# Attention scores in 64-key blocks side by side, with a PSUM bank of their own, in a fused recurrence and feed-forward kernel

## The chip, the cores and the metric

The kernel runs on one core of one Trainium2 chip. The time is the device time of one execution in microseconds. The kernel before takes 698.79 us (median of 3 runs, 698.2 to 699.16). A core has a matrix engine (TensorE, in the profile PE for its matmuls and PEld for its weight loads), VectorE (DVE), ScalarE (ACT), GpSimd (POOL) and SyncE (SP, which issues most DMAs here). TensorE writes into PSUM, eight banks of 512 fp32 values on each of 128 partitions; DVE and ACT read them out.

## What is computed

```python
# per batch (4), head (8): 768 tokens, 48 features
a = (a_re + i a_im) * min(|a|, 0.999) / (|a| + 1e-6)
for t in range(S):
    state = diag(a[t]) @ state + outer(k[t], v[t])     # complex
    y[t]  = q[t] @ Re(state)
x   = y as (3072 tokens, 384)
out = (x @ w_a) * (x @ w_b) @ w_out                     # d_ff = 1536
```

The running product of the decays turns the recurrence into causal attention in chunks: with q and k scaled by the products up to their token (real and imaginary part stacked, 96 rows a head), the scores of a chunk are k·q for keys not later than the query, plus a state that carries the earlier chunks.

## The kernel before

A unit is one chunk of 128 tokens for two batches; there are 12 units, 6 chunks by 2 pairs of batches. For each unit three kinds of work follow one another:

- *Preparation* (`prep`, `scale`): DVE and ACT make the scaled q and k of the unit in `qk`; SP's DMAs (`stack`, L352) restack them to 96 rows a head in `stk`. DVE's stream of 128x768 and 128x1536 operations is here.
- *Attention* (`attn`), in pieces, for the two batches i of the unit and for the two groups hg of four heads. `scores` (L380): four fp32 matmuls, keys by queries 128x128, into one PSUM tile of the pool `ps_m` (two banks, which `transposes` and `state` use too), then DVE multiplies by the causal mask into `am` (L388). `transposes` (L392): keys of four heads to token rows, copied by ACT into `kt` (L400). `outputs` (L403): v times masked scores, plus the state times q, into `xp`; these matmuls use 32 columns of the array each, four column groups side by side (L425, `tile_position`). ACT rounds `xp` into `xh`, DVE makes the rest `xl` (L429, L434). `state` (L436): kt times v (L442), added to the state `us` by DVE (L449).
- *Feed-forward* of the unit: for each of 12 blocks f of d_ff, `gemm1` (L480) makes a and b in one PSUM tile of the pool `ps_ab` (three banks) with 18 matmuls of rounded fp32 (L486); ACT copies a out (L494), DVE multiplies (L495), ACT and DVE split the product into `hh` and `hl` (L496, L497), and `gemm2` (L500) adds six matmuls (L504) into the two output banks.

The feed-forward of unit w, the attention of unit w+1 and the preparation of unit w+3 run in one loop over f; `attn` is a generator that hands out its pieces in the list `order` (L455, and L459 for unit 0), one or more per slot of the loop. The attention of unit 0 stands alone ahead of the loop. In the first 120 us the weights are also converted, with two matmuls each (L150, L151) into a bank of `ps_ab` or `ps_m`.

A scheduler of the framework puts the instructions of each engine in order, by priority and by its own estimate of when operands are ready. `tc.high_priority(offset=...)` moves the reading of PSUM forward: ATTN_FIRST for the masks and copies of the attention, MOE_FIRST for the feed-forward. On the chip each engine works off its queue in that order, and a waiting instruction holds up all behind it.

Each v tile (L360, 128 tokens by 4 pairs of heads by 128 columns) holds an even head in the first 64 columns of a pair and an odd one in the other 64.

Of the kernel before, what the change touches and what calls it, by code (L numbers as in the profile page):

```python
# [70 lines left out]
def tile_kernel(ctx: ExitStack, tc: tile.TileContext, a_d, qk_d, v_d, w_d, qn_d, kn_d, vn_d, an_d, out_d):  # L71
# [9 lines left out]
    vpool = fast.enter_context(tc.tile_pool(name="vpool", bufs=2))  # L81
    kvp = fast.enter_context(tc.tile_pool(name="kvp", bufs=2))
    moe = fast.enter_context(tc.tile_pool(name="moe", bufs=2))
    ps_ab = fast.enter_context(tc.tile_pool(name="ps_ab", bufs=3, space=PSUM))
    ps_o = fast.enter_context(tc.tile_pool(name="ps_o", bufs=1, space=PSUM))
    ps_x = fast.enter_context(tc.tile_pool(name="ps_x", bufs=1, space=PSUM))
    ps_m = fast.enter_context(tc.tile_pool(name="ps_m", bufs=2, space=PSUM))


    ident = const.tile([128, 128], F32, name="ident")  # L90
    make_identity(nc, ident)
    mask = const.tile([128, 128], F32, name="mask")
    nc.gpsimd.memset(mask, 1.0)
    nc.gpsimd.affine_select(out=mask, in_=mask, pattern=[[1, 128]], compare_op=ALU.is_ge,
                            fill=0.0, base=0, channel_multiplier=-1)
    biases = const.tile([128, 6], F32, name="biases")
    b_tiny, b_sq, b_eps, b_one, b_inv, b_rsq = (biases[:, i:i + 1] for i in range(6))
    vec.memset(b_tiny, TINY)
# [32 lines left out]
    def split_weights():  # L131
        for f in range(NF):
            for m, (c0, n) in enumerate(WPART):
                raw = raws[f, m]
                t = moe.tile([128, n], F32, name="o_sb", bufs=O_BUFS)
                tu = t.bitcast(U32)
                vec.tensor_scalar(out=tu, in0=raw[:, :, 1], scalar1=3, scalar2=0x3FFFFFFF,
                                  op0=ALU.logical_shift_left, op1=ALU.bitwise_and)
                vec.scalar_tensor_tensor(out=tu, in0=raw[:, :, 0], scalar=29, in1=tu,
                                         op0=ALU.logical_shift_right, op1=ALU.bitwise_or)  # L140
                vec.scalar_tensor_tensor(out=tu, in0=raw[:, :, 1], scalar=0xC0000000, in1=tu,  # L141
                                         op0=ALU.bitwise_and, op1=ALU.bitwise_or)
                w_t[f, m] = wpool.tile([128, 2, n], F32, name=f"w{m}{f}")
                hi, lo = w_t[f, m][:, 0], w_t[f, m][:, 1]
                act.copy(out=r(hi), in_=t)
                if f < CONV_ON_AB:
                    lp = ps_ab.tile([128, 512], F32, name="ab")
                else:
                    lp = ps_m.tile([128, 512], F32, name="pm")
                pe.matmul(out=lp[:, 0:n], lhsT=ident, rhs=t, start=True, stop=False)  # L150
                pe.matmul(out=lp[:, 0:n], lhsT=r(nident), rhs=r(hi), start=False, stop=True)  # L151
                act.copy(out=r(lo), in_=lp[:, 0:n])
            yield
# [49 lines left out]
    def prep(u):  # L203
# [52 lines left out]
        cc, bb = c_t[:], b_t[:]  # L256

        def joined(out, x, y, n):
            pb = small.tile([128, 2, 2, NG], F32, name="pb")
            vec.tensor_tensor(out=pb[:, :, :, 0:n], in0=x,  # L260
                              in1=y.unsqueeze(1).broadcast_to([128, 2, 2, n]), op=ALU.mult)
            vec.tensor_tensor(out=out, in0=pb[:, :, 0, 0:n], in1=pb[:, :, 1, 0:n], op=ALU.add)
# [108 lines left out]
    def attn(u, xh, xl):  # L371
# [7 lines left out]

        def scores(i, hg):  # L380
            qs, ks = cols(i)
            sp = ps_m.tile([128, 4, 128], F32, name="pm")
            for h4 in range(4):
                h = hg * 4 + h4
                pe.matmul(out=sp[:, h4], lhsT=stk[:, h, ks], rhs=stk[:, h, qs], start=True, stop=True)  # L385
            am = kvp.tile([128, 512], F32, name="am", bufs=2).rearrange("p (h t) -> p h t", h=4)
            with tc.high_priority(offset=ATTN_FIRST):
                vec.tensor_tensor(out=am, in0=sp, in1=mask[:].unsqueeze(1).broadcast_to([128, 4, 128]),  # L388
                                  op=ALU.mult)
            ams[i, hg] = am  # L390

        def transposes(i, hg):  # L392
            qs, ks = cols(i)
            tp = ps_m.tile([128, 512], F32, name="pm")
            for h4 in range(4):
                pe.transpose(out=tp[:, h4 * KS:(h4 + 1) * KS], in_=stk[0:KS, hg * 4 + h4, ks],  # L396
                             identity=ident[0:KS, 0:KS])
            kt = kvp.tile([128, 4, KS], F32, name="kt", bufs=2)
            with tc.high_priority(offset=ATTN_FIRST):
                act.copy(out=kt.rearrange("p h k -> p (h k)"), in_=tp[:, 0:4 * KS])  # L400
            kts[i, hg] = kt

        def outputs(i, half):  # L403
# [32 lines left out]
        def state(i, hg):  # L436
# [10 lines left out]
            with tc.high_priority(offset=ATTN_FIRST):  # L447
# [4 lines left out]
                if rescaled(c):  # L452
                    vec.tensor_tensor(out=uv, in0=uv, in1=sv, op=ALU.mult)

        order = [(scores, 0, 0), (scores, 0, 1), (transposes, 0, 0), (transposes, 0, 1),  # L455
                 (outputs, 0, 0), (outputs, 0, 1), (scores, 1, 0), (residual, 0, 0), (state, 0, 0), (scores, 1, 1),
                 (state, 0, 1), (transposes, 1, 0), (transposes, 1, 1), (outputs, 1, 0),
                 (outputs, 1, 1), (state, 1, 0), (residual, 1, 0), (state, 1, 1)]
        if u == 0:  # L459
            order = [(scores, 0, 0), (scores, 0, 1), (outputs, 0, 0), (outputs, 0, 1), (scores, 1, 0), (scores, 1, 1),  # L460
                     (residual, 0, 0), (outputs, 1, 0), (outputs, 1, 1), (transposes, 0, 0), (transposes, 0, 1),
                     (residual, 1, 0), (state, 0, 0), (state, 0, 1), (transposes, 1, 0), (transposes, 1, 1),
                     (state, 1, 0), (state, 1, 1)]
        for fn, i, g in order:
            if not (last and fn in (transposes, state)):
                fn(i, g)
# [297 lines left out]
```

## Time and profile before

| | us |
|---|---|
| median of 3 runs (lowest, highest) | 698.79 (698.2, 699.16) |
| the profiled execution, its own time | 698.89 |
| span of its profile | 697.2 |
| PE busy, whole span | 655.2 |
| DVE busy | 551.8 |
| ACT busy | 308.9 |
| matmuls of the scores (L385): 384 passes, mean length of one | 0.279 |
| matmuls of the outputs (L425): 768 + 640 passes, mean | 0.277, 0.273 |
| mask (L388): 48 on DVE, mean | 0.685 |
| copy of kt (L400): 40 on ACT, mean | 0.477 |

A matmul's length in a profile runs from its start to its modelled end, and matmuls are pipelined: one starts long before the one ahead has ended. What PE really spends on a run of matmuls is seen from the distance between starts, or in the chain of work that ended last, where each row lasts until the next one takes over. "Idle before" in the groups of lines is time in which an engine had nothing running, with the engine and line that ended it. The 40 slices show each engine's busy share in tenths.

### The profile page before, as it was taken

What the parts mean: (1) busy time and instruction counts of PE and PEld (TensorE: products, weight loads), DVE (VectorE), ACT (ScalarE), POOL (GpSimd) and SP (SyncE); (2) the same over time, 40 slices, a digit from 0 to 9 for tenths busy, and PEclk for the clock granted to TensorE, in tenths of its full rate; (3) what the DMA queues carried; (4) which work ended last, traced back from release to release, by engine and by line L of the source; (5) the groups of instructions that cost most, each with busy time, mean ns of one, the idle gap of its engine ahead of it and who ended that gap; (6) DMA issues with size and microseconds to landing.
All of it is one profiled execution on the core that took longest, in us unless ns stands there. A gap on an engine that the chain in (4) does not pass through costs nothing.

```text
span 697.2 us, 14316 instructions
## 1 busy us (share of the span) xinstructions
PE 655.2 (94%) x5854; PEld 610.8 (88%) x5854; DVE 551.8 (79%) x1241; ACT 308.9 (44%) x618; POOL 5.6 (1%) x11
## 2 busy tenths in 40 slices
PE   3557999999999999999999999999999999999996
PEld 1224889899899999999999999999999999999996
DVE  5999899988888889989899898999989853232221
ACT  6357755634535445245363554535542332221221
POOL 3000000000000000000000000000000000000000
PEclk9567999999999999999999999999999999999999
DMA  8973202411414205134151340511510500400000
GB/s 312 402 291 108 79 1 54 129 55 55 128 42 130 81 28 149 60 98 129 25 160 46 102 134 1 169 67 47 145 46 2 165 25 17 106 24 2 24 1 28
DMA packets 32088, 63.94 MB, mean 92 GB/s; under 512 B 3984, under 2 KB 10640, under 8 KB 32016
## 3 DMA queue, kind: packets, MB, share of 16 engines
q1 hardware_dynamic: 28560, 58.23, 27.0%
q10 hardware_dynamic: 3456, 4.72, 1.9%
q8 instruction: 48, 0.79, 0.5%
q14 instruction: 24, 0.20, 0.1%
HBM read 39.32 MB, written 4.72 MB: 63 GB/s over the span
## 4 chain that ended last, share of the span: by engine, by line
PE 64%; DVE 27%; ACT 4%; DMA 2%; issue 1%; SPq 1%; ACTq 0%; DVEq 0%
PE ab L486 30%; PE o L504 14%; PE xp L425 6%; PE pm L385 5%; PE pm L442 4%; DVE a_t L292 3%; DVE pr L230 2%; DVE qk L312 2%; DVE h_t L495 2%; PE pm L396 2%; DVE hl L497 2%; PE pm L150 2%; DVE z L297 2%; DVE pb L260 1%; DVE z L236 1%
## 5 line engine op out<-in xcount | busy, mean ns | idle before, releaser
L486 PE MATMUL ab<-xh,w 128*128 128x256 f32 x1728 | 339.0, 285 | 0.0
L486 PEld LDWEIGHTS ab<-xh,w 128*128 128x128 f32 x1728 | 278.1, 190 | 1.8 <-issue 1.4
L486 PE MATMUL ab<-xl,w 128*128 128x256 f32 x864 | 245.1, 284 | 0.0
L486 PEld LDWEIGHTS ab<-xl,w 128*128 128x128 f32 x864 | 164.4, 190 | 0.5 <-issue 0.2
L504 PE MATMUL o<-w,hh 128*128 128x384 f32 x576 | 152.3, 344 | 0.0
L494 ACT COPY h_t<-ab 128x256 f32<-128x256 f32 x144 | 53.1, 369 | 176.9 <-PE ab L486 176.8
L495 DVE TENSOR_TENSOR h_t<-ab,h_t 128x256 f32<-128x256 f32 x144 | 60.5, 420 | 72.5 <-ACT h_t L494 72.3
L504 PEld LDWEIGHTS o<-w,hh 128*128 128x128 f32 x576 | 96.8, 190 | 3.7 <-issue 3.0
L504 PE MATMUL o<-w,hl 128*128 128x384 f32 x288 | 96.9, 336 | 0.0
L496 ACT CAST hh<-h_t 128x256 fp32r<-128x256 f32 x144 | 58.0, 403 | 81.1 <-DVE h_t L495 80.9
L497 DVE TENSOR_TENSOR hl<-h_t,hh 128x256 fp32r<-128x256 f32 x144 | 60.5, 420 | 17.5 <-ACT hh L496 17.3
L150 PE MATMUL ab<-o_sb,ident 128*128 128x384 f32 x42 | 29.1, 794 | 29.9 <-DVE o_sb L141 29.8
L385 PE MATMUL pm<-stk 128*128 128x128 f32 x384 | 54.4, 279 | 2.7 <-DMA stk<-qk 2.7
L504 PEld LDWEIGHTS o<-w,hl 128*128 128x128 f32 x288 | 54.1, 188 | 0.0
L385 PEld LDWEIGHTS pm<-stk 128*128 128x128 f32 x384 | 48.7, 191 | 5.9 <-issue 4.8
L230 DVE TENSOR_TENSOR pr<-z 128x384 f32<-128x384 f32 (+1 forms) x91 | 47.1, 524 | 2.4 <-ACT z L216 0.8
L150 PEld LDWEIGHTS ab<-o_sb,ident 128*128 128x128 f32 x42 | 10.2, 286 | 39.8 <-DVE o_sb L141 29.4
L292 DVE TENSOR_TENSOR a_t<-z,b_t 128x768 f32<-128x768 f32 x48 | 44.6, 952 | 0.1
L425 PE MATMUL xp<-am,v_t 128*32 128x128 f32 x768 | 42.5, 277 | 1.3 <-DVE am L388 1.2
L312 DVE TENSOR_TENSOR qk<-qk,z 128x1536 f32<-128x1536 f32 (+1 forms) x28 | 42.7, 1524 | 0.1
L388 DVE TENSOR_TENSOR am<-pm,mask 128x512 f32<-128x512 f32 x48 | 32.8, 685 | 5.0 <-PE pm L385 4.8
L425 PE MATMUL xp<-stk,u 128*32 128x128 f32 x640 | 34.4, 273 | 0.0
(106 smaller groups left out, 761.7 us busy)
## 6 DMA issues: line engine op xcount, KB each, us to landing
w<-in_dram SPq DMA_DIRECT2D x36, 384.0 KB, 8.1
qk<-in_dram SPq DMA_DIRECT2D x12, 768.0 KB, 4.8
a_t<-in_dram SPq DMA_DIRECT2D x11, 768.0 KB, 4.3
stk<-qk SPq DMA_DIRECT2D x42, 192.0 KB, 3.3
v_t<-in_dram SPq DMA_DIRECT2D x24, 256.0 KB, 2.7
out_dram<-o_sb ACTq DMA_DIRECT2D x24, 192.0 KB, 1.9
stk<-qk SPq DMA_DIRECT2D x18, 192.8 KB, 3.4
stk<-qk SPq DMA_DIRECT2D x14, 128.0 KB, 3.1
```

What stands on the lines that cost most here:

```text
L150: pe.matmul(out=lp[:, 0:n], lhsT=ident, rhs=t, start=True, stop=False)
L230: vec.tensor_tensor(out=pr[:, :, :, o:o + n], in0=view(zz, W + at_(i) + 2 * o, [[W, 2], [-W, 2], [2, n]]), in1=tok(slice(1, 3), i - 1, o, ...
L292: vec.tensor_tensor(out=pz[:, s].rearrange("p (j b e) -> p j b e", j=SUB // 2, e=2), in0=zb[:, 1 + s], in1=view(bb, (1 + k - s) * NB, [[0, ...
L312: vec.tensor_tensor(out=qk4[:, :, k, x0:x1], in0=qk4[:, :, 1, x0:x1], in1=z[:, k].rearrange("p (j t) -> p j t", j=NJ).unsqueeze(2).broadca ...
L385: pe.matmul(out=sp[:, h4], lhsT=stk[:, h, ks], rhs=stk[:, h, qs], start=True, stop=True)
L425: pe.matmul(out=xp[qd * 32:(qd + 1) * 32, ti], lhsT=l, rhs=rr, start=st, stop=sp_, tile_position=(0, qd * 32), skip_group_check=True)
L486: pe.matmul(out=ab[:, m * TOK:(m + 1) * TOK], lhsT=r(w_ab(f, part, m * NJ + i)), rhs=r(xt[:, i, :]), start=n == 0, stop=n == 8)
L494: act.copy(out=h_t, in_=ab[:, 0:TOK])
L495: vec.tensor_tensor(out=h_t, in0=ab[:, TOK:2 * TOK], in1=h_t, op=ALU.mult)
L496: act.copy(out=r(hh), in_=h_t)
L497: vec.tensor_tensor(out=r(hl), in0=h_t, in1=hh, op=ALU.subtract)
L504: pe.matmul(out=os_[tt][:, 0:DM], lhsT=r(ht[:, ts]), rhs=r(w_t[f, 2][:, part, :]), start=(f == 0 and n == 0), stop=(f == NF - 1 and n == 2))
```

## The change

Scores are made in two blocks b of 64 keys. Block 0 meets all 128 queries, block 1 only the queries 64 to 127; the block of later keys and earlier queries is left out. Each matmul uses 64 columns of the array, and an even and an odd head work in the two column halves at once: half g = b xor x, x being 0 for the even head. An odd head's two halves of keys therefore land exchanged on the partitions. So the mask gets a second, exchanged form for odd heads; the v tile is loaded with the halves of the odd heads exchanged (three DMAs instead of one), and `kt` is copied in three pieces. All scores go into one PSUM tile `sp` that is made once, set to zero, and kept: the part left out stays zero. Its bank is taken from `ps_ab`, which has two left. The weight conversions up to block 6 alternate between the pools' banks, a small buffer `pb` goes from two to one, and the lists of pieces in `attn` are put in another order.

```diff
-    ps_ab = fast.enter_context(tc.tile_pool(name="ps_ab", bufs=3, space=PSUM))
+    ps_ab = fast.enter_context(tc.tile_pool(name="ps_ab", bufs=2, space=PSUM))
...
+    ps_s = fast.enter_context(tc.tile_pool(name="ps_s", bufs=1, space=PSUM))
...
-    mask = const.tile([128, 128], F32, name="mask")
+    mask = const.tile([128, 2, 128], F32, name="mask")
     nc.gpsimd.memset(mask, 1.0)
-    nc.gpsimd.affine_select(out=mask, in_=mask, pattern=[[1, 128]], compare_op=ALU.is_ge,
-                            fill=0.0, base=0, channel_multiplier=-1)
+    for rows, base in ((mask[:, 0], 0), (mask[:, 1], 64), (mask[0:64, 1], -64)):
+        nc.gpsimd.affine_select(out=rows, in_=rows, pattern=[[1, 128]], compare_op=ALU.is_ge,
+                                fill=0.0, base=base, channel_multiplier=-1)
+    sp = ps_s.tile([128, 4, 128], F32, name="sp")
+    vec.memset(sp, 0.0)
...
-                if f < CONV_ON_AB:
+                if f < CONV_ON_AB and (NJ * f + m) % 4 < 2:
...
-            pb = small.tile([128, 2, 2, NG], F32, name="pb")
+            pb = small.tile([128, 2, 2, NG], F32, name="pb", bufs=1)
...
-            sync.dma_start(out=t, in_=v_d[u, i])
+            tv, dv = (x.rearrange("p (g x e) -> p g x e", x=2, e=64) for x in (t, v_d[u, i]))
+            sync.dma_start(out=tv[:, :, 0], in_=dv[:, :, 0])
+            for g in range(2):
+                sync.dma_start(out=tv[64 * g:64 * (g + 1), :, 1], in_=dv[64 * (1 - g):64 * (2 - g), :, 1])
...
-            sp = ps_m.tile([128, 4, 128], F32, name="pm")
-            for h4 in range(4):
-                h = hg * 4 + h4
-                pe.matmul(out=sp[:, h4], lhsT=stk[:, h, ks], rhs=stk[:, h, qs], start=True, stop=True)
+            for h4 in (0, 2):
+                for b in range(2):
+                    for x in range(2):
+                        h, g = hg * 4 + h4 + x, b ^ x
+                        pe.matmul(out=sp[64 * g:64 * (g + 1), h4 + x, 64 * b:],
+                                  lhsT=stk[:, h, ks.start + 64 * b:ks.start + 64 * (b + 1)],
+                                  rhs=stk[:, h, qs.start + 64 * b:qs.stop], start=True, stop=True,
+                                  tile_position=(0, 64 * g), skip_group_check=True)
...
-                act.copy(out=kt.rearrange("p h k -> p (h k)"), in_=tp[:, 0:4 * KS])
+                act.copy(out=kt[:, 0::2], in_=tv[:, 0::2])
+                for g in range(2):
+                    act.copy(out=kt[64 * g:64 * (g + 1), 1::2], in_=tv[64 * (1 - g):64 * (2 - g), 1::2])
...
-        order = [(scores, 0, 0), (scores, 0, 1), (transposes, 0, 0), (transposes, 0, 1),
+        order = [(scores, 0, 0), (transposes, 0, 0), (scores, 0, 1), (transposes, 0, 1),
                  (outputs, 0, 0), (outputs, 0, 1), (scores, 1, 0), (residual, 0, 0), (state, 0, 0), (scores, 1, 1),
-                 (state, 0, 1), (transposes, 1, 0), (transposes, 1, 1), (outputs, 1, 0),
-                 (outputs, 1, 1), (state, 1, 0), (residual, 1, 0), (state, 1, 1)]
+                 (state, 0, 1), (outputs, 1, 0), (transposes, 1, 0), (outputs, 1, 1), (residual, 1, 0),
+                 (transposes, 1, 1), (state, 1, 0), (state, 1, 1)]
```

Line numbers of the changed program are higher: L393 are the matmuls of the scores (before L385), L399 the mask (L388), L408 the transposes (L396), L413 and L415 the copies of kt (L400), L440 the outputs (L425), L457 the state's matmuls (L442), L501 and L519 the two products of the feed-forward (L486, L504), L510 and L512 DVE's part of it (L495, L497).

How the order on the engines changes shows at three places. First PE in the attention of unit 10, from the last matmul of a block's first product to the next one: the scores of both head groups of batch 0, the second product, the transposes. Before:

```order
L486 MATMUL ab<-xh,w_757 128x256
L385 MATMUL pm<-stk 128x128 x8
L504 MATMUL o_6766<-w_482,hh 128x384 x2
L504 MATMUL o_6766<-w_482,hl 128x384
L504 MATMUL o_6767<-w_482,hh 128x384 x2
L504 MATMUL o_6767<-w_482,hl 128x384
L396 MATMUL pm<-ident,stk 128x96 x8
L486 MATMUL ab<-xh,w_827 128x256
```

And in the changed program:

```order
L501 MATMUL ab<-xh,w_792 128x256
L393 MATMUL sp<-stk 64x128 x2
L393 MATMUL sp<-stk 64x64 x2
L393 MATMUL sp<-stk 64x128 x2
L393 MATMUL sp<-stk 64x64 x2
L408 MATMUL pm<-ident,stk 128x96 x4
L519 MATMUL o_7009<-w_493,hh 128x384 x2
L519 MATMUL o_7009<-w_493,hl 128x384
L519 MATMUL o_7010<-w_493,hh 128x384 x2
L519 MATMUL o_7010<-w_493,hl 128x384
L393 MATMUL sp<-stk 64x128 x2
```

The two calls of scores were eight matmuls in a row; now they are two runs of eight, with half of the transposes and the second product between them, and the second writes the same tile `sp`.

Then PE some 10 us later in the same attention, around the last call of scores. Before:

```order
L442 MATMUL pm<-v_t,kt 96x48 x4
L385 MATMUL pm<-stk 128x128 x4
L504 MATMUL o_6766<-w_767,hh 128x384 x2
L504 MATMUL o_6766<-w_767,hl 128x384
L504 MATMUL o_6767<-w_767,hh 128x384 x2
L504 MATMUL o_6767<-w_767,hl 128x384
L442 MATMUL pm<-v_t,kt 96x48 x4
L396 MATMUL pm<-ident,stk 128x96 x4
```

And now:

```order
L457 MATMUL pm<-v_t,kt 96x48 x4
L393 MATMUL sp<-stk 64x128 x2
L393 MATMUL sp<-stk 64x64 x2
L393 MATMUL sp<-stk 64x128 x2
L393 MATMUL sp<-stk 64x64 x2
L519 MATMUL o_7009<-w_802,hh 128x384 x2
L519 MATMUL o_7009<-w_802,hl 128x384
L519 MATMUL o_7010<-w_802,hh 128x384 x2
L519 MATMUL o_7010<-w_802,hl 128x384
L457 MATMUL pm<-v_t,kt 96x48 x4
L440 MATMUL xp<-am,v_t 32x128 x4
```

The call stands at the same place, between state and second product; behind the state the outputs in 32-column groups follow where the transposes did.

Last DVE, at the masks of batch 0 of unit 8. Before:

```order
L306 TENSOR_TENSOR a_t<-a_t 128x768
L495 TENSOR_TENSOR h_t<-ab,h_t 128x256
L388 TENSOR_TENSOR am<-pm,mask 128x512 x2
L497 TENSOR_TENSOR hl<-h_t,hh 128x256
L322 TENSOR_TENSOR a_t<-a_t 128x768
```

And now:

```order
L310 TENSOR_TENSOR a_t<-a_t 128x768
L510 TENSOR_TENSOR h_t<-ab,h_t 128x256
L399 TENSOR_TENSOR am<-sp,mask 128x512
L512 TENSOR_TENSOR hl<-h_t,hh 128x256
L399 TENSOR_TENSOR am<-sp,mask 128x512
L326 TENSOR_TENSOR a_t<-a_t 128x768
```

The two masks stood together; now hl stands between them, and the second one follows a call of scores that itself has to follow the first mask.

More of the change, by code (lines that the diff above doesn't have):

```diff
@@ L381, in scores @@
             qs, ks = cols(i)
-            sp = ps_m.tile([128, 4, 128], F32, name="pm")
-            for h4 in range(4):
-                h = hg * 4 + h4
-                pe.matmul(out=sp[:, h4], lhsT=stk[:, h, ks], rhs=stk[:, h, qs], start=True, stop=True)
+            for h4 in (0, 2):
[6 more added lines that the diff above has]
+                                  tile_position=(0, 64 * g), skip_group_check=True)
             am = kvp.tile([128, 512], F32, name="am", bufs=2).rearrange("p (h t) -> p h t", h=4)
             with tc.high_priority(offset=ATTN_FIRST):
-                vec.tensor_tensor(out=am, in0=sp, in1=mask[:].unsqueeze(1).broadcast_to([128, 4, 128]),
+                vec.tensor_tensor(out=am.rearrange("p (r x) t -> p r (x t)", x=2), in0=sp.rearrange("p (r x) t -> p r (x t)", x=2),
+                                  in1=mask.rearrange("p x t -> p (x t)").unsqueeze(1).broadcast_to([128, 2, 256]),
                                   op=ALU.mult)
@@ L398, in transposes @@
             kt = kvp.tile([128, 4, KS], F32, name="kt", bufs=2)
+            tv = tp[:, 0:4 * KS].rearrange("p (h k) -> p h k", k=KS)
             with tc.high_priority(offset=ATTN_FIRST):
-                act.copy(out=kt.rearrange("p h k -> p (h k)"), in_=tp[:, 0:4 * KS])
+                act.copy(out=kt[:, 0::2], in_=tv[:, 0::2])
+                for g in range(2):
+                    act.copy(out=kt[64 * g:64 * (g + 1), 1::2], in_=tv[64 * (1 - g):64 * (2 - g), 1::2])
             kts[i, hg] = kt
@@ L453, in state @@
                     vec.tensor_tensor(out=uv, in0=uv, in1=sv, op=ALU.mult)
-        order = [(scores, 0, 0), (scores, 0, 1), (transposes, 0, 0), (transposes, 0, 1),
+        order = [(scores, 0, 0), (transposes, 0, 0), (scores, 0, 1), (transposes, 0, 1),
                  (outputs, 0, 0), (outputs, 0, 1), (scores, 1, 0), (residual, 0, 0), (state, 0, 0), (scores, 1, 1),
-                 (state, 0, 1), (transposes, 1, 0), (transposes, 1, 1), (outputs, 1, 0),
-                 (outputs, 1, 1), (state, 1, 0), (residual, 1, 0), (state, 1, 1)]
+                 (state, 0, 1), (outputs, 1, 0), (transposes, 1, 0), (outputs, 1, 1), (residual, 1, 0),
+                 (transposes, 1, 1), (state, 1, 0), (state, 1, 1)]
         if u == 0:
[L460 to L463, printed above, removed]
+            order = [(scores, 0, 0), (transposes, 0, 0), (scores, 0, 1), (transposes, 0, 1), (scores, 1, 0),
+                     (outputs, 0, 0), (outputs, 0, 1), (residual, 0, 0), (scores, 1, 1),
+                     (state, 0, 0), (outputs, 1, 0), (outputs, 1, 1), (residual, 1, 0), (state, 0, 1),
+                     (transposes, 1, 0), (transposes, 1, 1), (state, 1, 0), (state, 1, 1)]
         for fn, i, g in order:
```

## The prediction

> **What bounds the kernel now.** First the page: its busy shares, then the 40 slices.
>
> ```profile
> PE 655.2 (94%) x5854; PEld 610.8 (88%) x5854; DVE 551.8 (79%) x1241; ACT 308.9 (44%) x618; POOL 5.6 (1%) x11
> PE   3557999999999999999999999999999999999996
> DVE  5999899988888889989899898999989853232221
> PE 64%; DVE 27%; ACT 4%; DMA 2%; issue 1%; SPq 1%; ACTq 0%; DVEq 0%
> ```
>
> PE is full from the fifth slice (some 75 us) to the end. DVE stands beside it up to slice 32, and holds 27% of the chain, so a busy PE alone proves little. The chain read in order of time decides. Here is unit 10's attention, the stretch from 572.6 us: start, length, what, number of passes. An fp32 matmul runs as two passes (the groups of lines below count 384 for 192 matmuls of L385), so four heads' scores are x8.
>
> ```profile
> 572.59 2.15 PE ab L486 x18
> 574.73 1.78 PE pm L385 x16
> 576.52 1.04 PE o L504 x6
> 577.56 0.66 PE pm L396 x8
> 578.23 2.17 PE ab L486 x18
> 580.40 1.89 PE xp L425 x64
> 582.28 1.27 PE o L504 x6
> 583.55 0.89 PE pm L385 x8
> 584.44 2.15 PE ab L486 x18
> 586.59 0.64 PE pm L442 x8
> 587.23 0.96 PE pm L385 x8
> 588.19 1.05 PE o L504 x6
> ```
>
> No row is another engine's and no time is missing between rows: PE issues without a pause. What is added to PE's stream here lengthens the kernel by as much. Earlier units mix DVE rows into the chain, but PE's real pauses there are few. The groups of lines give the largest, a wait for the stacked operands:
>
> ```profile
> L385 PE MATMUL pm<-stk 128*128 128x128 f32 x384 | 54.4, 279 | 2.7 <-DMA stk<-qk 2.7
> L388 DVE TENSOR_TENSOR am<-pm,mask 128x512 f32<-128x512 f32 x48 | 32.8, 685 | 5.0 <-PE pm L385 4.8
> L400 ACT COPY kt<-pm 128x384 f32<-128x384 f32 x40 | 18.8, 477 | 24.2 <-PE pm L396 24.1
> L451 ACT COPY u<-pm 96x192 f32<-96x192 f32 x8 | 2.5, 316 | 1.8 <-PE pm L442 1.6
> ```
>
> So I price the change by PE's stream in units 1 to 11, which run beside the feed-forward; unit 0 runs before it and is priced apart.
>
> **Scores: the passes themselves.** Before, 16 passes took 1.78 us, so 0.111 us each and 0.89 us for a call of four heads. Now four heads times two key blocks are 8 matmuls, 16 passes, each with 64 columns of weights, half of them over 128 queries and half over 64. Two column groups work side by side, so there are 8 rounds of two passes. The only work of before in column groups is L425 (32 columns, four groups, 128 queries):
>
> ```profile
> 580.79 0.40 PE L425 MATMUL xp<-am,v_t 128*32 128x128 f32 x8
> 581.01 0.40 PE L425 MATMUL xp<-stk,u 128*32 128x128 f32 x8
> ```
>
> Eight passes, two rounds of four, begin every 0.22 us: 0.109 us a round for 128 queries, with the groups really side by side. A round over 64 queries is not in the trace. It lies between 0.055 (half of the streaming) and 0.109 (no gain); L442's 96 columns over 48 queries took 0.64/8 = 0.080 a pass, so loading 64 columns needs some 0.053, and I take 0.057. A call is then 4 x 0.109 + 4 x 0.057 = 0.66 us, a gain of 0.23 us, and **44 calls in units 1 to 11 give -10.1 us**. If the 64-query rounds cost 0.109, the gain is 0.02 a call.
>
> **Scores: entering and leaving the column groups.** In the chain above the 64 passes of L425 are 16 rounds, 16 x 0.109 = 1.74 us, but took 1.89, and the six L504 behind them took 1.27 instead of 1.04. That is 0.15 us on the way in and 0.23 on the way out. The visit of 64 passes in the next unit reads the same, with L486 behind it:
>
> ```profile
> 628.12 1.89 PE xp L425 x64
> 630.00 2.35 PE ab L486 x18
> ```
>
> 0.15 + 0.20 = 0.35. I take **0.34 us a visit**. L385 needs none: 0.89 between L504 and L486. The Trainium skill, "TensorEngine Tiling (Array Packing)", section Key Properties, says that a change of the tiling mode, unlike a change of tile, drains the array; it gives no price, and by it the new scores must pay as L425 does. The trace agrees for L425.
>
> Visits are counted along PE's order in units 1 to 11: 40 before, all L425. In the changed order every call of scores stands between full-width work, as in the pieces of order shown with the change: 88 visits, and 10 direct steps between 64- and 32-column work. Unit 10 has 3 before and 7 after. 48 more visits x 0.34 = **+16.3 us**. A direct step costs between nothing and a visit; between these I take 0.15, **+1.5 us** (0 to 3.4). A 64-column load cannot start before the switch either and is 0.027 us longer than a 32-column one (0.080/96 x 32): 59 x 0.027 = **+1.6 us**. In units 1 to 3 nine pairs of heads are cut after their first matmul by other work, so that one of two groups idles for two rounds of 0.109: 9 x 0.22 = **+2.0 us**. Some of all this falls into the 2.7 us in which PE waits for the stacked operands in units 2 and 3: **-2.5 us** (0 to -2.7).
>
> **One bank for all scores.** A call now waits until DVE has masked the call before. Behind the waiting matmul stands PE's whole queue. In unit 8 DVE is latest:
>
> ```profile
> 472.28 1.95 PE L385 MATMUL pm<-stk 128*128 128x128 f32 x16
> 474.88 1.28 DVE L388 TENSOR_TENSOR am<-pm,mask 128x512 f32<-128x512 f32 x2
> 475.61 1.15 PE L396 MATMUL pm<-ident,stk 96*128 96x96 f32 x8 [0.34 <-DVE am L388]
> ```
>
> The first mask would end at 474.88 + 0.69 = 475.57. PE, with the transposes (0.33), six L504 (1.05) and a visit between the calls, wants the bank at about 472.28 + 0.66 + 0.34 + 0.33 + 1.05 = 474.7: a wait of 0.9. In unit 10 DVE starts the mask at once, and there is none. Between 0 and 0.9 for 11 units I take the end that most units are near: **+1.0 us** (0 to 10). DVE's second mask now stands behind hl in its order and holds up what follows until PE comes; DVE has idle time to cover it. The windows, by stretch: PE, PEld, DVE, ACT, POOL busy, clock, DMA share, GB/s:
>
> ```profile
> 450.00:500.00 50.00, 49.61 (x487) 47.99 (x487) 47.58 (x107) 25.27 (x49) 0.00 (x0) 1.00 0.26 80
> 500.00:550.00 50.00, 49.87 (x492) 48.53 (x490) 46.06 (x115) 16.31 (x36) 0.00 (x0) 1.00 0.22 61
> ```
>
> DVE is idle for 2.4 and 3.9 of 50 us, about a unit's length; gone, each further microsecond would be PE's.
>
> **Two banks for the first product.** A bank must be drained before the group after next. The tightest of the 144 groups:
>
> ```profile
> 157.75 0.28 PE L486 MATMUL ab<-xh,w 128*128 128x256 f32 x1
> 162.56 0.42 DVE L495 TENSOR_TENSOR h_t<-ab,h_t 128x256 f32<-128x256 f32 x1
> 164.14 0.28 PE L486 MATMUL ab<-xh,w 128*128 128x256 f32 x1
> ```
>
> The group of 157.75 is drained at 162.98, the group after next starts at 164.14: 1.16 us to spare, so **0**. If DVE is later by more than that, PE waits for the difference.
>
> **The rest.** The copy of kt becomes three; a copy of half the width took 0.316 us, so 0.95 instead of 0.48, 40 times +0.47 = 19 us of ACT, which is 44% busy: 0, and 0.5 us a transpose where ACT is late for h_t. The v tiles come in 72 DMAs instead of 24; SP waits for DVE 35.1 us before the operands' DMAs, so their issue is hidden:
>
> ```profile
> SPq L352 <- DVE qk L312: 35.1, 2, 31.2
> ```
>
> The memset, wider mask and the split of the conversions over four banks lie in the first 75 us, where DVE is full with other work: 0. Unit 0 has 11 visits instead of 6, +1.7, less 4 x 0.23 and what hides in its waits for DVE and DMA: **+0.5 us** (-2 to +3).
>
> **Sum**, against the profiled execution (698.89 us: span 697.2 and 1.7 around it; the median of the runs is 698.79, so nothing is corrected): -10.1 + 16.3 + 1.5 + 1.6 + 2.0 - 2.5 + 1.0 + 0.5 = +10.3. **709.2 us**, slower by 1.5%.
>
> **Rivals.**
> - *Forecast*, 58%: 704 to 716.
> - *Entering 64-column work costs little* (for it: only 32-column visits are in the trace; against: the delay looks like emptying the array and loading anew, whatever the width). Without a price for the 59 runs of scores, what remains is -10.1 + 2.0 - 2.5 + 1.0 + 0.5 = -9.1, so **690 us, faster**, 10%. It decides at some 0.16 us a visit: the 9.1 less 1.5 for the direct steps, over 48 visits. Half the price everywhere (8.2 + 0.8 + 0.8 in place of 16.3 + 1.5 + 1.6) gives 699.5, 8%.
> - *The two groups do not work side by side* (the change doesn't do what it says): the order of the groups is 0, 1, 1, 0, and the same group twice running is not in the trace; L425 always goes round all four. If a second matmul of one group holds back the other, or loads are not hidden, a call is 1.1 to 1.33 us: +9 to +19 on the forecast, 718 to 729, 14%. The Trainium skill, "TensorE: Matmul & The Clock Gate", section The mechanism, has loads overlap running matmuls only in other row groups; these share one, so each pass would also pay its load. L425's rounds of 0.109 in one row group speak against it.
> - *Waits take over*: scores wait for the mask and the first product for its bank in most units, +0.5 to +0.9 for 11 units beside the 1.0: 714 to 720, 10%.
>
> **Range and chances.** 699 to 724 takes in the forecast, half price, waits and half of the third rival. A measurement here tells 0.2% (1.4 us) from no change. Faster is the free entry and part of half price, 0.14; same 0.05; slower 0.81.
>
> **What would show it.** In the changed chain: L393 runs of x16 at about 0.8 us with 0.2 us more on the matmuls behind them confirm both prices; at 0.66 and no tail the second case holds; above 1.1 the third. A wait of L393 for DVE, or of L501 for DVE, is the fourth. PE's stream in units 9 and 10 should grow by 0.4 to 0.8 us each, the plain last unit by nothing; if unit 11's plain stretch grows, I have missed something in the feed-forward.

## The result and the profile after

The changed kernel takes **713.93 us** (median of 4 runs, 713.82 to 714.33), the kernel before 698.5 (4 runs, 697.94 to 699.16): ratio **1.0222**, 95% interval 1.0204 to 1.0239. The profiled execution has a span of 712.1 us (before 697.2).

The page of the changed kernel first: busy shares of two engines, their 40 slices with the granted clock, the chain's shares by engine, and the groups that the change made.

```profile
PE 669.2 (94%) x6238; PEld 612.5 (86%) x6238; DVE 553.8 (78%) x1242; ACT 329.4 (46%) x698; POOL 6.5 (1%) x13
PE   3656999999999999999999999999999999999996
DVE  6999699888798798989899898998989963233221
PEclk9575799999999999999999999999999999999998
PE 74%; DVE 18%; DMA 3%; ACT 2%; issue 1%; SPq 1%; ACTq 0%; DVEq 0%
L393 PE MATMUL sp<-stk 128*64 128x128 f32 (+1 forms) x768 | 52.6, 262 | 2.7 <-DMA stk<-qk 2.3
L399 DVE TENSOR_TENSOR am<-sp,mask 128x512 f32<-128x512 f32 x48 | 32.9, 686 | 17.8 <-PE sp L393 15.1
```

PE's share of the chain grew from 64% to 74%. The mask costs DVE what it did (32.9 us), but DVE's idle time ahead of it went from 5.0 to 17.8 us, nearly all of it waiting for scores. The granted clock reads 5 and 7 in the fourth and fifth slices, where before had 7 and 9:

```profile
PEclk9567999999999999999999999999999999999999
```

The chain of waits in unit 10's attention, to be read against the chain of unit 10 in the prediction (start, length, what, passes):

```profile
590.10 0.82 PE sp L393 x16
590.91 0.48 PE pm L408 x4
591.39 2.16 PE ab L501 x18
593.55 1.89 PE xp L440 x64
595.44 1.24 PE o L519 x6
596.68 0.82 PE sp L393 x16
597.50 2.34 PE ab L501 x18
```

A call of scores lasts 0.82 us where 0.66 + 0.15 was forecast, and the 18 passes of L501 behind it take 2.34 instead of 2.15. In this place the prices of the pass and of the visit fit, the two column halves do work side by side, and entering 64-column work is not free.

The starts of the feed-forward's first products, changed kernel less before (read off the trace), say where the 14 us came: +5.3 us at block 8 of unit 0's feed-forward, behind unit 0's attention; +10.0 at the first block of unit 1's; +12.3 at that of unit 3's, some 250 us into the run; and only +1.8 more to the last product, of which the feed-forward stretches of units 9 and 10 have 0.39 and 0.57 and unit 11's 0.14. So the last units look much as forecast (how much of that is the blocks' is said further below), and the first 250 us lost far more. There DVE waits. Its waits ahead of masks from 57 to 300 us (operation, whom it waits for, us in total, times, longest), before:

```profile
DVE am L388 <- PE pm L385: 3.7, 6, 0.9
```

and changed:

```profile
DVE am L399 <- PE sp L393: 10.6, 8, 2.7
DVE am L399 <- PE xp L440: 2.5, 1, 2.5
```

And TensorE's clock is low. A window of 15 us (busy PE, PEld, DVE, ACT, POOL, clock, DMA share, GB/s) over unit 0's attention, before:

```profile
65.00:80.00 15.00, 14.00 (x156) 11.66 (x155) 13.71 (x24) 8.83 (x19) 0.00 (x0) 1.00 0.40 125
```

and changed:

```profile
65.00:80.00 15.00, 14.10 (x106) 10.59 (x105) 9.44 (x15) 6.18 (x14) 0.00 (x0) 0.51 0.33 107
```

PE counts as just as busy, but at half clock it did 106 instructions instead of 156, and DVE was busy 4.3 us less.

### The profile page after: what moved, and what is told of

Same layout as the page of the kernel before. It is cut to its first block, busy times and chain, and to the rows that moved or that the text cites. A ratio compares the mean times of both kernels' runs of the same rounds, so it can differ in the third digit from the quotient of the medians.

```text
span 712.1 us, 15260 instructions
## 1 busy us (share of the span) xinstructions
PE 669.2 (94%) x6238; PEld 612.5 (86%) x6238; DVE 553.8 (78%) x1242; ACT 329.4 (46%) x698; POOL 6.5 (1%) x13
## 4 chain that ended last, share of the span: by engine, by line
PE 74%; DVE 18%; DMA 3%; ACT 2%; issue 1%; SPq 1%; ACTq 0%; DVEq 0%
PE ab L501 35%; PE o L519 18%; PE xp L440 7%; PE sp L393 7%; PE pm L457 4%; PE pm L408 3%; DMA stk<-qk 2%; DVE a_t L296 2%; DVE pr L234 2%; PE pm L154 1%; DVE qk L316 1%; DVE h_t L510 1%; DVE hl L512 1%; DVE o_sb L143 1%; DVE z L240 1%
## 5 line engine op out<-in xcount | busy, mean ns | idle before, releaser
L501 PE MATMUL ab<-xh,w 128*128 128x256 f32 x1728 | 338.8, 285 | 0.0
L501 PEld LDWEIGHTS ab<-xh,w 128*128 128x128 f32 x1728 | 276.2, 189 | 3.6 <-issue 2.4
L501 PE MATMUL ab<-xl,w 128*128 128x256 f32 x864 | 243.6, 282 | 0.0
L501 PEld LDWEIGHTS ab<-xl,w 128*128 128x128 f32 x864 | 162.7, 188 | 0.8 <-issue 0.4
L519 PE MATMUL o<-w,hh 128*128 128x384 f32 x576 | 153.5, 346 | 0.0
L510 DVE TENSOR_TENSOR h_t<-ab,h_t 128x256 f32<-128x256 f32 x144 | 60.4, 420 | 70.4 <-ACT h_t L509 69.8
L519 PEld LDWEIGHTS o<-w,hh 128*128 128x128 f32 x576 | 97.3, 188 | 4.0 <-issue 2.4
L519 PE MATMUL o<-w,hl 128*128 128x384 f32 x288 | 97.7, 339 | 0.0
L512 DVE TENSOR_TENSOR hl<-h_t,hh 128x256 fp32r<-128x256 f32 x144 | 60.5, 420 | 19.6 <-ACT hh L511 19.3
L393 PE MATMUL sp<-stk 128*64 128x128 f32 (+1 forms) x768 | 52.6, 262 | 2.7 <-DMA stk<-qk 2.3
L519 PEld LDWEIGHTS o<-w,hl 128*128 128x128 f32 x288 | 54.2, 188 | 0.3 <-issue 0.2
L393 PEld LDWEIGHTS sp<-stk 128*64 128x64 f32 x768 | 41.4, 141 | 14.8 <-issue 7.0
L399 DVE TENSOR_TENSOR am<-sp,mask 128x512 f32<-128x512 f32 x48 | 32.9, 686 | 17.8 <-PE sp L393 15.1
L154 PE MATMUL ab<-o_sb,ident 128*128 128x384 f32 x22 | 17.7, 910 | 27.8 <-DVE o_sb L145 27.8
L440 PE MATMUL xp<-am,v_t 128*32 128x128 f32 x768 | 42.5, 282 | 0.0
L457 PEld LDWEIGHTS pm<-v_t,kt 128*96 128x96 f32 x320 | 33.4, 170 | 2.6 <-ACT kt L415 1.2
L457 PE MATMUL pm<-v_t,kt 128*96 128x48 f32 x320 | 34.0, 250 | 0.9 <-ACT kt L415 0.9
```

Of the source, the lines that this page charges most:

```text
L393: pe.matmul(out=sp[64 * g:64 * (g + 1), h4 + x, 64 * b:], lhsT=stk[:, h, ks.start + 64 * b:ks.start + 64 * (b + 1)], rhs=stk[:, h, qs.star ...
L440: pe.matmul(out=xp[qd * 32:(qd + 1) * 32, ti], lhsT=l, rhs=rr, start=st, stop=sp_, tile_position=(0, qd * 32), skip_group_check=True)
L457: pe.matmul(out=kp[0:KS, h4 * D:(h4 + 1) * D], lhsT=kts[i, hg][:, h4, :], rhs=v_t[:, o:o + D], start=True, stop=True)
L501: pe.matmul(out=ab[:, m * TOK:(m + 1) * TOK], lhsT=r(w_ab(f, part, m * NJ + i)), rhs=r(xt[:, i, :]), start=n == 0, stop=n == 8)
L510: vec.tensor_tensor(out=h_t, in0=ab[:, TOK:2 * TOK], in1=h_t, op=ALU.mult)
L512: vec.tensor_tensor(out=r(hl), in0=h_t, in1=hh, op=ALU.subtract)
```

## The experiments

First the parts were undone one by one. Theory A held that two thirds of the loss come from the conversions, which now share the pm banks with unit 0's transposes; theory B that it is the visits and blocks.

**1. Conversions on the ab banks again, all else as changed.**

```diff
-                if f < CONV_ON_AB and (NJ * f + m) % 4 < 2:
+                if f < CONV_ON_AB:
```

> The changed kernel (713.9 us) with one line undone: the conversions of the first seven weight blocks go to the ab banks again, none of them to the pm banks. Theory A (two thirds of the loss come from the conversions that now share the pm banks with unit 0's transposes: they run late, TensorE has too little to do around 60 us, and its granted clock falls to 0.5): the granted clock is back at 0.9 to 1.0 from 65 us on, the first product of block 6 starts some 5 us earlier, unit 1's attention may win some of its 4.6 us, and the whole is 704 to 709. Theory B (the loss is the visits to column groups and the new orders with one sp bank; the conversions are beside it): 712.5 to 715.

Measured 709.25 us, ratio to before 1.0144 (1.0127 to 1.0161): 4.7 us less than the changed kernel. But block 6 starts only 0.6 us earlier, and the clock over unit 0 is not back:

```profile
65.00:80.00 15.00, 14.03 (x110) 9.69 (x109) 9.60 (x17) 8.11 (x18) 0.00 (x0) 0.66 0.34 107
```

The size is at the upper end of theory A, its reason doesn't fit: the clock has little to do with the conversions.

**2. Full-width scores, all else as changed.**

```diff
-            for h4 in (0, 2):
-                for b in range(2):
...
+            for h4 in range(4):
+                h = hg * 4 + h4
+                pe.matmul(out=sp[:, h4], lhsT=stk[:, h, ks], rhs=stk[:, h, qs], start=True, stop=True)
...
+                act.copy(out=kt.rearrange("p h k -> p (h k)"), in_=tp[:, 0:4 * KS])
...
+            sync.dma_start(out=t, in_=v_d[u, i])
```

> The changed kernel with the scores again as one 128x128 product a head (plain mask, plain loads of v, one copy of kt), but with its own sp bank, two ab banks, the new orders and the split conversions. Theory A (the blocks cost about 4 us, as the steady units grew; the rest is the start): 708 to 711, the start of block 6's first product within 1 us of the changed kernel's, and about 0.5 us off each of the two units that wait for nothing but TensorE. Theory B (48 more visits at 0.34 us, less 10 us saved, is the loss itself, and the start is the blocks' too): 701 to 704.

704.12 us, ratio 1.0076 (1.0059 to 1.0093): 9.8 us less than the changed kernel. Theory A is wrong here: the blocks are the larger part, and 4.5 us of the start are theirs (block 6 starts 0.8 us after before's, not 5.3).

**3. The kernel before, with the split of the conversions alone.** (The edit of experiment 1 the other way round.)

> The kernel before (698.5 us) with one line of the change alone: the conversions of the first seven blocks alternate between the ab banks (three, as before) and the pm banks. Theory A: they come late and the start loses 3 to 8 us, 701.5 to 706.5, with a lower granted clock between 60 and 80 us. Theory B: 698 to 699.5, nothing.

704.63 us, ratio 1.0089 (1.0072 to 1.0106): the split alone costs 5.7 us. The granted clock from 65 to 80 us is 0.96, so again it isn't the clock. Two rows of PE's timeline of this kernel show what it is:

```profile
117.76 0.34 PE L504 MATMUL o<-w,hl 128*128 128x384 f32 x1
119.51 0.91 PE L150 MATMUL pm<-o_sb,ident 128*128 128x384 f32 x2 [1.41 <-DVE o_sb L141]
```

PE waits 1.41 us for DVE to put together a weight piece. The windows from 110 to 130 us of this kernel and, below, of before:

```profile
110.00:130.00 20.00, 18.37 (x99) 14.80 (x97) 19.77 (x39) 11.56 (x23) 0.00 (x0) 1.00 0.42 120
```

```profile
110.00:130.00 20.00, 20.00 (x123) 17.80 (x122) 19.67 (x37) 11.63 (x22) 0.00 (x0) 1.00 0.42 118
```

DVE is full in both; PE loses 1.6 us of 20. Before, 21 conversions had started by 66 us; with the split 19, since two pieces of block 6 now want pm banks and run behind unit 0's attention, from 80 us on. Every later piece, and DVE's work on it, slides into a stage in which DVE has no room: block 10's first product starts at 122.8 instead of 119.6 us, though block 8's had started 1.8 us earlier than before.

**4. Both undone:** own sp bank, two ab banks and the new orders remain.

> Both undone: the changed kernel with full-width scores and with the conversions on the ab banks; what is left of the change are the own sp bank, two ab banks and the orders. Theory A: 698 to 702, about the kernel before. Theory B: 701 to 704, the same as with full-width scores alone. A third view (orders and the single sp bank are the loss): 707 to 713.

698.62 us, ratio 0.9992 (0.9983 to 1.0002). The bank, the two ab banks and the orders together cost nothing. The four kernels make a square: the blocks cost 10.6 us with the conversions on ab (709.25 - 698.62) and 9.8 without (713.93 - 704.12); the split costs 4.7 with blocks and 5.5 with full-width scores. The two add up to within 0.8 us (10.6 + 5.5 against 15.3 for both).

**5. Only block 6's conversions back on the ab banks**, those of blocks 0 to 5 split as changed.

```diff
-                if f < CONV_ON_AB and (NJ * f + m) % 4 < 2:
+                if f < CONV_ON_AB and (f == CONV_ON_AB - 1 or (NJ * f + m) % 4 < 2):
```

> The changed kernel (713.9 us) with only the three conversions of weight block 6 on the ab banks; those of blocks 0 to 5 alternate as changed. Theory A (the price of the split is that two pieces of block 6 queue behind unit 0's attention and push all later ones back into the stage in which VectorE has no room): 708.5 to 710, as with all of them undone. Theory B (the alternation of blocks 0 to 5 over four banks costs as well, since they wait for each other's copies in another order): 711.5 to 714.

709.91 us (5 runs, 709.86 to 713.37), ratio 1.0158 (1.0141 to 1.0175). The late pieces of block 6 are 4.0 of the split's 4.7 us. One run of five, the profiled one, was at 713.4, so places of loss are not read from its profile.

**6. Visits alone:** both undone, and one product of 64 columns by 8 ahead of each call of full-width scores in units 1 to 11, which the scores overwrite.

```diff
+            if u > 0:
+                pe.matmul(out=sp[0:64, 0, 0:8], lhsT=stk[:, hg * 4, ks.start:ks.start + 64],
+                          rhs=stk[:, hg * 4, qs.start:qs.start + 8], start=True, stop=True,
+                          tile_position=(0, 0), skip_group_check=True)
```

> Full-width scores with the conversions on the ab banks (698.6 us), and in units 1 to 11 one extra product of 64 columns by 8 ahead of each of the 44 groups of scores, overwritten by the scores: 44 more visits to column groups and nothing else. Forecast price (0.36 us a visit, all of it on TensorE's path): 714 to 715. Theory A (the price holds, about 0.35 us a group in the trace, but half of it is hidden in units 3 to 8, whose end VectorE or the loads set as well): 704 to 709. Rival (a visit is nearly free and the blocks lose by their own loads and passes): 698 to 700.

713.72 us, ratio 1.0212 (1.0195 to 1.023): 15.1 us for 44 visits, **0.343 us a visit**. As a mean over the kernel, and with the two short passes of the extra product in it, that is the forecast's price of 0.34; the visit alone is somewhat less. The total of my later theory was too low. Its chain shows both halves of the price, the way in within the 0.21 of the extra product, the way out in 1.09 instead of 0.89 for the scores behind:

```profile
594.85 0.21 PE sp L387 x2
595.07 1.09 PE sp L392 x8
```

That is 0.41 a visit where PE waits for nothing, and the mean hides a spread. Against experiment 4, feed-forward stretch by stretch, the four visits of a unit cost 0.20 to 0.22 us each in the stretches of units 6 to 8, and 0.27 to 0.56 in the others. So in the middle about half does hide, as the theory had it. What it hides in is seen in PE's waits of experiment 4 from 300 to 560 us, where full-width scores wait for the mask of the call before, at four places in units 5 to 8:

```profile
PE sp L388 <- DVE am L391: 1.9, 4, 0.8
```

With the extra products 0.3 us of these waits are left.

Then, where the blocks lose. All with the conversions on the ab banks, so 698.62 us is none of the blocks and 709.25 all of them.

**7. Blocks in units 1 to 11, unit 0 full-width.**

```diff
+            if u == 0:
+                for h4 in range(4):
+                    h = hg * 4 + h4
+                    pe.matmul(out=sp[:, h4], lhsT=stk[:, h, ks], rhs=stk[:, h, qs], start=True, stop=True)
-            for h4 in (0, 2):
+            for h4 in (0, 2) if u else ():
```

> The changed kernel with the conversions on the ab banks (709.25 us), and with unit 0 alone computed by full-width scores; units 1 to 11 keep the blocks. Theory A (unit 0's attention loses some 4.5 us because the blocks and their changes of mode keep TensorE's granted clock at 0.5 to 0.7 until 79 us): the clock is at 1.0 from 68 us on, block 6's first product starts 4 us earlier, and the whole is 704 to 705.5. Theory B (the loss of unit 0 is made up later in any case, since VectorE bounds the units after it): 708 to 709.5.

708.87 us, ratio 1.0133 (1.0115 to 1.0152). Block 6 starts 5.8 us earlier than with all blocks, the clock is at 1.00 from 65 us on, and yet all but 0.4 us is gone again by the end, as theory B had it. Its reason is not shown by that. The scheduler ordered this kernel's attention anew: in the stretch of unit 3, where unit 4's attention runs, PE enters column groups 12 times instead of 7 with all blocks, and that stretch is 3.8 us longer. The stretch ahead of it, 2.6 us longer, has a wait of 2.0 us for the stacked operands and, right behind it, 3.4 us of half clock (0.66 as a mean from 225 to 230 us).


**8. Blocks in units 4 to 11 alone** (the same edit with `u < 4`), where no other instruction cuts a call of scores.

> Conversions on the ab banks; units 0 to 3 full-width, blocks in units 4 to 11 alone, where no other instruction cuts a group of scores: 32 groups, 33 more visits to column groups than with full-width scores throughout (698.6 us). Theory A (in uncut groups the visit and the shorter passes cancel; the 10 us of the blocks are those of unit 0 and of the cut groups of units 1 to 3): 698.4 to 700. Theory B (the forecast's prices hold in every unit, 0.46 us net a unit, and about as much again for what the visit adds behind the group): 702 to 706.

699.79 us, ratio 1.0015 (1.0006 to 1.0025): eight units of blocks cost 1.2 us. In unit 10 the 16 passes take the same 0.82 us as in the changed kernel, visit included:

```profile
583.86 0.82 PE sp L400 x16
584.68 2.34 PE ab L515 x18
```

**9. Blocks in unit 0 alone.**

> Conversions on the ab banks; blocks in unit 0 alone, units 1 to 11 full-width (698.6 us with full-width throughout). Theory A (unit 0's attention loses 4 to 6 us for good, at a granted clock of 0.5 to 0.7 until 79 us): 702.5 to 705. Theory B (what is lost there is made up in units 1 to 3, whose loads arrive no earlier): 698.5 to 700.

707.65 us (4 runs, 705.84 to 715.64), ratio 1.0154 (1.0091 to 1.0217). More than either theory said, and the widest spread of all kernels here. The window over unit 0, and DVE's waits ahead of masks from 57 to 300 us:

```profile
65.00:80.00 15.00, 14.02 (x108) 9.61 (x108) 9.62 (x18) 8.15 (x18) 0.00 (x0) 0.65 0.34 107
```

```profile
DVE am L407 <- PE sp L395: 5.0, 7, 1.6
DVE am L410 <- PE sp L400: 2.4, 1, 2.4
DVE am L410 <- PE xp L454: 2.1, 1, 2.1
```

Blocks in unit 0 alone cost 9.0 us, in units 1 to 11 alone 10.3, in both 10.6, in units 4 to 11 alone 1.2. These don't add: unit 0 and units 1 to 3 seem to cost the same nine us in two ways (the 9.0 is the median of a wide spread). What they share was looked for in DVE's time, worked out from the gaps between its instructions in the one profiled execution of each kernel:

| kernel (conversions on ab unless said) | time (median), us | end of unit 4's scaling of k on DVE, us | DVE idle up to there, us | DVE's waits ahead of masks, 57 to 300 us |
|---|---|---|---|---|
| full-width throughout | 698.62 | 262.3 | 26.5 | 4.6 |
| blocks in units 4 to 11 | 699.79 | 262.0 | 26.1 | 4.7 |
| blocks in unit 0 | 707.65 | 266.6 | 30.2 | 9.5 |
| blocks in units 1 to 11 | 708.87 | 271.9 | 35.2 | 10.4 |
| blocks in all units | 709.25 | 271.1 | 34.7 | 11.1 |
| the changed kernel (conversions split) | 713.93 | 274.1 | 37.4 | 13.1 |

DVE's preparation runs units ahead of the rest. By the end of unit 4's it is late by about as much as it stood idle: 8.8 and 8.2 us from the first row to the fifth, of which the waits ahead of masks are 6.5. The masks stand in DVE's queue between the preparation's operations, and a mask that waits for scores holds the preparation up. In units 0 to 3 the scores come late, in unit 0 at half clock, in units 1 to 3 because transposes and other work stand between the eight matmuls of a call: in the changed kernel's trace the passes of a unit's four calls, from start to start, take 5.0 us of PE in units 2 and 3 (before 3.8 and 3.6), and 3.3 in units 4, 5, 10 and 11.

Two things limit this account. With blocks in unit 0 alone DVE is only 4.3 us late, and the time is 9.0 us longer. And PE's own order offers a second account for units 1 to 3: with blocks in all units their cut calls make 32 visits to column groups, full-width 13. At 0.343 us the 19 more are 6.5 us (shorter passes and direct steps left out), and the three stretches in which these units' attention runs grew by 6.9 from experiment 4 to experiment 1. (In the eight stretches behind them 31 more visits, less what the shorter passes save, come to -0.2 us in all, with part of the price hidden in PE's waits for masks.) Which of the two carries the loss, or how they share it, these runs don't tell apart.

**10. Calls of scores held together as one piece for the scheduler.**

```diff
+            with tc.tile_critical():
-            for h4 in (0, 2):
+                for h4 in (0, 2):
```

> Blocks in all units and the conversions on the ab banks (709.25 us), with the eight products of a group of scores held together as one piece for the scheduler, so that no transposes or states stand between them: in units 0 to 3 TensorE's order has 6, 9, 7 and 7 visits to column groups where it had 10, 7, 11 and 14, and a group takes 0.82 us everywhere instead of 1.25. Theory A (the 9 us that the blocks cost beyond the uncut units are the cut groups in units 0 to 3, through VectorE, whose masks wait for them): 700 to 704, and VectorE's idle time ahead of the masks up to 300 us falls from 11 us to about 6. Theory B (whatever cuts them, the scores of units 0 to 3 arrive late because the operands do, and the holding together only moves the wait to TensorE): 707 to 711.

870.83 us, ratio 1.246 (1.2431 to 1.2488). It says nothing on the question. Holding the piece together makes it wait for more than its operands, as the groups of this kernel show:

```profile
L400 DVE TENSOR_TENSOR am<-sp,mask 128x512 f32<-128x512 f32 x48 | 33.2, 692 | 150.4 <-PEq L389 145.6
```

PE's sequencer waits at the line of the piece (L389), at 45 of 48 masks, and DVE for it. So that it is the masks' waits on DVE which carry the loss of units 0 to 3 is what the table in part goes along with; it was not shown by taking them away, and cut calls that pay for more visits on PE stay a rival.

**11 and 12. Fewer visits.** In the first version the second half's scores follow the outputs of the first in one visit, with two sp banks and one pm bank throughout:

```diff
-    ps_m = fast.enter_context(tc.tile_pool(name="ps_m", bufs=2, space=PSUM))
+    ps_m = fast.enter_context(tc.tile_pool(name="ps_m", bufs=1, space=PSUM))
...
+    sps = [ps_s.tile([128, 4, 128], F32, name=f"sp{t}") for t in range(2)]
...
+                 (outputs, 0, 0), (outputs, 0, 1), (scores, 1, 0), (scores, 1, 1), (residual, 0, 0), (state, 0, 0),
```

> A version with fewer visits: conversions on the ab banks, full-width scores in units 0 to 2, blocks in units 3 to 11; the sp bank becomes two and the pm banks one, and the scores of both groups follow each other, those of the second half right behind the outputs of the first, so that the last units have 3 visits to column groups where the change has 6. By the measured prices: 0.9 us less a unit in score passes and 0.36 + 0.45 us more in visits and steps between 32 and 64 columns, so 697 to 699 if one pm bank is enough for the start; if it isn't, 700 to 706.

703.69 us, ratio 1.0066 (1.0049 to 1.0083): no gain. The feed-forward stretches of units 1 to 3 last 3.4, 2.3 and 3.4 us longer than with full-width scores throughout; there one pm bank serves all transposes and states, and the calls of units 3 and 4 are cut (which of these it is was not tried apart). But those of units 9 and 10 are 0.56 and 1.14 us shorter (0.43 and 0.64 against the kernel before). So the second version keeps full-width scores and two pm banks up to unit 4, and only then turns one pm bank into the second sp bank:

```diff
+        if w + 1 == 5:
+            early.close()
+            ps_m.pools = [ps_m1]
+            ps_s2 = fast.enter_context(tc.tile_pool(name="ps_s2", bufs=1, space=PSUM))
+            sps[1] = ps_s2.tile([128, 4, 128], F32, name="sq")
+            vec.memset(sps[1], 0.0)
```

> A version for speed: units 0 to 4 full-width with one sp bank and two pm banks; then one pm bank becomes a second sp bank, and units 5 to 11 use blocks with both groups' scores side by side in the order, the second half's right behind the outputs of the first: 3 or 4 visits to column groups a unit as before the change, and 16 products of scores a visit more. From the units in which the first merged version showed this (0.5 to 1.1 us less than full-width in five of seven): 694.5 to 697.5. Rival (the units in the middle are set by VectorE and the loads as well, and give it back): 698 to 700.

**696.81 us** (11 runs, 696.07 to 698.05), ratio **0.9975** (0.9965 to 0.9984): faster than both kernels, by 0.25% against before. Its chain in unit 10, where the scores of batch 1 follow the outputs of batch 0:

```profile
577.59 1.89 PE xp L467 x64
579.48 0.82 PE sp L413 x16
580.29 0.67 PE sq L413 x16
580.96 2.33 PE ab L534 x18
```

The 32 passes of both calls last 0.82 + 0.67 us, the second without a way in, and the way out, 0.18, is paid once on L534 behind them. Before, two calls took 1.78 and no visit. How much of the gain on the kernel before the blocks earn is not shown. In the traces this kernel is already 1.1 us ahead of before where the stretch of unit 4 starts, ahead of the first block, and 1.7 at the last product; and the new order with two sp banks was not run with full-width scores.

## Why the prediction came out

713.93 was measured, 709.2 forecast, within a range 25 us wide; the likeliest case was the right one. The two prices it rests on came out, as did the blocks' total. Where the blocks lose did not, so that the total is that near is partly luck; and one term put at nothing was 4.7 us. Point by point:

- **Visits, +16.3:** right as a mean. 0.343 us each over 44 visits (two short passes included), and 0.15 and 0.2 at the two ends as in the rows of before. It is not the same everywhere: 0.41 where PE waits for nothing, about 0.2 in the stretches of units 6 to 8. The Trainium skill, "TensorEngine Tiling (Array Packing)", section Key Properties, has a change of tiling mode drain the array; the runs agree and give the price.
- **Passes, -10.1:** 0.66 us for a call, as forecast: experiment 12 measures 0.67 for a call without a way in. The full-width call in its surroundings took 3.39/4 = 0.85 rather than 0.89, so the gain was a little smaller.
- **The blocks' sum**, -10.1 + 16.3 + 1.5 + 1.6 + 2.0 - 2.5 + 0.5 = +9.3: measured 9.8 and 10.6. But not where the prediction put it. It spread it over units 1 to 11; units 4 to 11 cost 1.2, units 0 to 3 the rest. Unit 0's +0.5 (-2 to +3) was 9.0 for that unit alone, and the cut pairs of units 1 to 3 carry more than their 2.0. "DVE has idle time to cover it" was read from windows at 450 to 550 us, and from 57 to 300 us the waits ahead of masks rose from 3.7 to 13.1 us. That too much in the later units and too little in the first ones nearly cancel is luck.
- **In the middle** (feed-forward of units 3 to 8, attention of units 4 to 9) a stretch grew by -0.07 to 0.29 us instead of some 0.5. The prediction added the visits to PE's stream as if PE never waited there, and quoted a row of unit 8 in which L396 waits 0.34 us for DVE's mask. In that stretch the transposes' share of PE fell from 1.65 to 1.31 us. The own bank alone doesn't win this: with full-width scores (experiment 4) the wait moves to the next call of scores, the 1.9 us shown at experiment 6, and the stretches of units 5 to 8 are 0.10 to 0.46 us longer than before. In the changed kernel PE waits less:

```profile
PE sp L393 <- DVE am L399: 0.5, 2, 0.3
```

- **Units 9 and 10**, which have no such wait, grew by 0.39 and 0.57, inside or at the edge of the 0.4 to 0.8 that the prediction named for visits and passes. But with full-width scores they had grown by 0.13 and 0.50 already; from experiment 4 to experiment 1 the blocks add only 0.27 and 0.08. That sign confirmed less than it seemed to.
- **Waits for the stacked operands, -2.5:** did not go. PE still waits 2.3 us for them (the row of L393); the loads come from a preparation that is itself late.
- **One bank, +1.0, and two ab banks, 0:** PE waited for masks 0.5 us in the changed kernel and by the list of its waits never for an ab bank; all of it with the orders is -0.3 us (0.9983 to 1.0002). Yet the prediction's own sign, that unit 11's plain stretch should not grow, did show something in the feed-forward: it is 0.14 to 0.15 us longer in each of the twelve traced kernels with two ab banks, and 0.00 longer in experiment 3, which has three. It grows evenly, by 0.013 us a block. Over 144 blocks that would be 1.9 us (an estimate: elsewhere it can't be told from the rest).
- **Conversions, 0:** this step failed. "DVE is full with other work: 0" was taken for cover; a full DVE is what makes a conversion that slips expensive. It cost 4.7 us, which happens to be as much as the forecast was short, 4.0 of it by the pieces of one block that had to queue behind unit 0's attention. The order of PE shows this without a run: 21 conversions by 66 us before, 19 after, and the next one at 85.
- **kt and v:** ACT's copies of kt took 37.8 us instead of 18.8 (the forecast 19 more), and PE waited for one of them once, 0.9 us: as good as nothing.
- **The rivals:** free entry and half price fall with 0.343; halves that don't work side by side would have made a call 1.1 us or more, it was 0.82, way in included. That rival was also summed wrongly: 1.1 to 1.33 instead of 0.66 over 44 calls is +19 to +29 on the forecast, 728 to 739 us; its +9 to +19 count from the 0.89 of before, and the range would not have held it. Waits took over, but DVE's for PE, not PE's for DVE as that rival had it.

## What to carry to other kernels

Price an array-mode visit by what changes mode on either side, not by the matmuls inside it: the one kernel with blocks that beat the kernel before, by 0.25%, is one in which a visit carries two calls or rides on one that was there already (how much of that is the order's was not tried). Count the visits in the order that results, not in the source: cut calls pay more than one. Where the engine waits in any case, part of the price is hidden, so a price that holds as a mean can be wrong in each unit. In a start-up stage where two engines are both full, look at which waiting instruction stands in whose queue, and count any step that leaves its place there; "full with other work" is a cost, not a cover. And a square of runs (each part undone, both undone) shows in four kernels whether two causes add, which the profile's places of loss did not.

## What the hardware showed unexpectedly

Blocks in unit 0 kept TensorE's granted clock low although PE counted as fully busy. Windows of the changed kernel, 2 us each:

```profile
71.00:73.00 2.00, 2.00 (x17) 1.83 (x16) 0.84 (x2) 0.57 (x2) 0.00 (x0) 0.50 0.96 345
73.00:75.00 2.00, 2.00 (x14) 1.21 (x17) 0.36 (x1) 0.02 (x1) 0.00 (x0) 0.50 0.87 304
75.00:77.00 2.00, 2.00 (x21) 1.58 (x22) 1.90 (x5) 0.93 (x3) 0.00 (x0) 0.50 0.08 31
77.00:79.00 2.00, 2.00 (x21) 1.71 (x21) 0.18 (x1) 1.57 (x2) 0.00 (x0) 0.50 0.00 0
79.00:81.00 2.00, 2.00 (x30) 1.64 (x30) 1.30 (x3) 1.00 (x5) 0.00 (x0) 0.82 0.00 0
```

The same work in full width, with the blocks undone and the conversions on ab (experiment 4), had the clock back much earlier:

```profile
65.00:67.00 2.00, 2.00 (x12) 1.74 (x12) 1.33 (x5) 2.00 (x4) 0.00 (x0) 0.83 0.16 25
67.00:69.00 2.00, 1.51 (x16) 1.33 (x15) 1.91 (x4) 1.43 (x5) 0.00 (x0) 1.00 0.88 297
```

The Trainium skill, "TensorE: Matmul & The Clock Gate", Part 1: The HAM clock gate, has the clock released after some 3.4 us of sustained work. In the first rows PE counts as busy from 71 to 79 us and the clock stays at 0.50; from 69 to 71 us it was busy for 1.10 of 2. The busy time of a matmul ends at a modelled end, so short gaps at each change of mode would not show in it; whether those gaps, the pause ahead, or half-used columns kept the clock low was not tried. That it goes with the blocks of unit 0 is shown by experiments 7 and 9, with 1.00 and 0.65 from 65 to 80 us. In the second of them, and in experiment 1, the clock was back for 3.4 us from 68 us on, and fell to 0.50 again until 79.
